# Making the decay tables of a chunked linear attention in place, by VectorE scans

## The chip, the cores and the metric

The kernel runs on one core of a Trainium2 chip. The metric is the device time of one execution in microseconds; the median of several runs is given. All data are float32.

## The reference

Two blocks follow each other. The first is a linear attention with decay (B=4, H=8 heads, S=768, D=64); the second, on the result x of shape (4, 768, 512), adds the real part of a two-dimensional Fourier transform, normalizes the rows and applies an MLP of width 2048. Cut to what matters:

```python
block = 64
rel = pos[:, None] - pos[None, :]
Dmask = np.where(rel >= 0, lam[:, None, None] ** rel[None], 0.0)   # lam: one number a head, 0.97 to 0.99
lam_pow = lam[:, None, None] ** (pos[None, :, None] + 1)
for b in range(nb):                                   # blocks of the sequence
    intra = (qb @ kb.T * Dmask) @ vb
    inter = (qb * lam_pow) @ kv_state
    out[block] = intra + inter
    kv_state = lam ** block * kv_state + (kb * lam ** (block - 1 - pos)).T @ vb
x = out as (B, S, H * D)
u = x + real(fft(fft(x, axis=1), axis=2))
un = (u - mean(u)) / sqrt(var(u) + 1e-6)              # over the 512 columns
result = u + relu(un @ w_ch1) @ w_ch2
```

The result doesn't depend on the block's size. The kernel uses blocks (chunks) of 128, so it needs, for each of the 8 heads h, the powers of lam[h] from 0 to 128.

## The kernel before

**Tables.** Three tables come out of lam. `decay` [128, 8, 128] holds, on partition j, lam[h]^(i-j) for i >= j and 0 else; it multiplies the transposed scores (`sc`, L295), and its last column `kpow` scales k for the state update (`kd`, L269, on GpSimd). `qpow` [128, 4, 128] holds lam[h]^(i+1) for the two heads of a pair, one on partitions 0 to 63 and one on 64 to 127; it multiplies the transposed q (`qs`, L283), and its last column `spow` scales the running state (L310).

They are made in L152 to L188. lam is read into eight partitions (`sq`, L154). VectorE doubles the number of known powers seven times, on eight partitions: a tensor_scalar extends the row `z` by its own length times lam^n (L159), and a tensor_tensor squares lam^n (L161). The row, 127 zeros, then powers 0 to 128, is stored to device memory (`zd`, L165). From there `qpow` is read by two DMAs that repeat a row on 64 partitions (L170), and `shifted` by one whose partitions start one element apart (L182). TensorE multiplies `shifted` by `flip`, the identity with reversed columns (L186), which turns the order of the partitions round, and ScalarE copies the two halves to `decay` (L187).

**Attention, `attn_chunk`.** For each batch, six chunks in order. A chunk loads k, q, v for all heads (L262, two buffers each, so the load of chunk c+2 waits until chunk c has let go of the buffer), transposes k and q on TensorE (L273, L278; copies to `kT`, `qT` by ScalarE, L275, L280), makes scores (L291), masks them (L295), updates the state (L306, L308 to L311), makes the output transposed (L319, L323, copied by L326), turns it back (L330) and copies it to `x` or `xn` (L333, L334). Parts of x are stored to device memory (`xa`, `xb`, L337 to L341), and gathered from there mirrored (L377 to L385, by indirect DMAs of GpSimd) for the fold with which the Fourier transform begins (L366 to L415).

**The rest.** `fft_ln` makes the Fourier transform by matmuls (L439, L452 to L457) and the normalization (L469 to L492). `mlp` runs four of the twelve pairs of row tiles through the two weight matrices (L554, L568), woven with the attention of the later batches; the other eight go through `late` in pairs, with seven products in place of eight (L636, L683).

**Weights.** They are loaded in 32 pieces of 512 KB (`raw`, L228). VectorE and ScalarE unpack each with seven instructions (L233 to L241). `raw` shares its five buffers with the MLP's hidden rows.

**Order.** The loads of k, q, v, `raw` and the tables of the Fourier transform are issued on one queue, SP's; the stores of `xa` and `xb` on ScalarE's. The program is written as generators that yield estimated durations, and `weave` interleaves them in proportion; the first batch's attention is woven with half of the first weight matrix:

```python
run(weave(attn(0), part(w, 0.5 * NW), 0.5 * NW / t_att))
```

Within that, a build-time planner orders each engine's queue, so an instruction need not be issued in its source order; where the order must hold, `keep_in_program_order` says so. [...]

Of the kernel before, what the change touches and what calls it, by code (L numbers as in the profile page):

```python
# [10 lines left out]
F32 = mybir.dt.float32  # L11
# [5 lines left out]
ALU = mybir.AluOpType  # L17
# [59 lines left out]
def kernel(  # L77
# [10 lines left out]
    nc = tc.nc  # L88
    B, H, S, D = q.shape
    DM = H * D  # L90
    DFF = moe_w_ch1.shape[1]
    C = 128
    NC = S // C
    HC = NC // 2
    HP = H // 2
# [10 lines left out]
    HD = [slice(0, 64), slice(64, 128)]  # L106
# [8 lines left out]
    def front_pool(name, bufs):  # L115
        return front_end.enter_context(tc.tile_pool(name=name, bufs=bufs, side="left"))
# [4 lines left out]
    const = front_pool("const", 1)  # L121
# [3 lines left out]
    fp = front_pool("fp", 1)  # L125
# [5 lines left out]
    dram = ctx.enter_context(tc.tile_pool(name="dram", bufs=1, space=bass.MemoryType.DRAM))  # L131
# [7 lines left out]
    def new(pool, shape, tag, **kw):  # L139
        cnt[0] += 1  # L140
        return pool.tile(shape, F32, tag=tag, name=f"{tag}{cnt[0]}", **kw)
# [4 lines left out]
    def psum_m(shape):  # L146
        return new(pm, shape, "pm")
# [1 line left out]

    z = fp.tile([H, 2 * C], F32, tag="fo0", name="z")  # L152
    sq = const.tile([H, 8], F32, name="sq")
    nc.sync.dma_start(sq[:, 0:1], lam.rearrange("(h o) -> h o", o=1))  # L154
    nc.vector.memset(z, 0.0)
    nc.vector.memset(z[:, C - 1:C], 1.0)
    n, b2 = 1, 0
    while n < C:
        nc.vector.tensor_scalar(z[:, C - 1 + n:C - 1 + 2 * n], z[:, C - 1:C - 1 + n],  # L159
                                sq[:, b2:b2 + 1], None, op0=ALU.mult)  # L160
        nc.vector.tensor_tensor(sq[:, b2 + 1:b2 + 2], sq[:, b2:b2 + 1], sq[:, b2:b2 + 1], op=ALU.mult)  # L161
        n, b2 = 2 * n, b2 + 1
    nc.vector.tensor_copy(z[:, 2 * C - 1:2 * C], sq[:, b2:b2 + 1])
    zd = dram.tile([H, 2 * C], F32, name="zd")
    nc.sync.dma_start(zd, z)  # L165
    z0 = zd[0:1, 0:1]

    qpow = const.tile([128, HP, C], F32, name="qpow")
    for hi in range(2):
        nc.sync.dma_start(  # L170
            qpow[HD[hi]],
            bass.AP(z0.tensor, z0.offset + hi * 2 * C + C, [[0, D], [4 * C, HP], [1, C]]))
    spow = qpow[:, :, C - 1:C]

    ident = const.tile([128, 128], F32, name="ident")
    make_identity(nc, ident)


    flip = fp.tile([128, 128], F32, tag="ds", name="flip")
    nc.vector.tensor_copy(flip, ident[:, ::-1])  # L180
    shifted = fp.tile([C, H, C], F32, tag="fe0", name="shifted")
    nc.sync.dma_start(shifted, bass.AP(z0.tensor, z0.offset, [[1, C], [2 * C, H], [1, C]]))  # L182
    decay = const.tile([C, H, C], F32, name="decay")
    for g in range(0, H, 4):
        ps = psum_m([C, 4, C])
        nc.tensor.matmul(ps, lhsT=flip, rhs=shifted[:, g:g + 4, :], start=True, stop=True)  # L186
        nc.scalar.copy(decay[:, g:g + 4, :], ps)  # L187
    kpow = decay[:, :, C - 1:C].broadcast_to([C, H, D])  # L188

    cvt = const.tile([128, 1], F32, name="cvt")  # L190
# [627 lines left out]
```

## Time and profile before

| | us |
|---|---|
| median of 8 runs | 876.17 (873.32 to 881.85) |
| profiled execution | 876.15 |
| its span | 874.4 |
| PE (matmul) busy | 802.0 (92%) |
| DVE busy | 436.1 (50%) |
| ACT busy | 179.1 (20%) |
| POOL busy | 82.5 (9%) |
| mean granted TensorE clock | 0.982 of full speed |

The span runs from the first to the last instruction of the profile; 1.75 us of the execution lie around it. PE is TensorE's matmuls, PEld its weight loads, DVE is VectorE, ACT ScalarE, POOL GpSimd, SP the queue of SyncE. A line such as L295 is a line of the kernel. Where a row of the timeline has a bracket, it gives how long the engine was idle before the instruction, and what ended that. [...]

### The profile page before, as it was taken

How to read it: one execution, taken by the hardware profiler on the slowest of the kernel's cores; microseconds unless marked ns; L12 is line 12 of the kernel's file. 1: busy time of each engine (PE TensorE's matmuls, PEld its weight loads, DVE VectorE, ACT ScalarE, POOL GpSimd, SP SyncE). 2: the span in 40 equal slices, each digit the busy share in tenths (PEclk: the TensorE clock that was granted, in tenths of full speed). 3: DMA queues.
4: the chain of work that ended last, by engine and by line, in shares of the span. 5: the costliest groups of instructions: out<-in, count | busy, mean ns of one | idle time of the engine just before them, and what ended most of it. 6: DMA issues, size and time to landing. Idle time of an engine off the chain costs nothing.

```text
span 874.4 us, 11679 instructions
## 1 busy us (share of the span) xinstructions
PE 802.0 (92%) x4596; PEld 638.7 (73%) x4596; DVE 436.1 (50%) x1022; ACT 179.1 (20%) x419; POOL 82.5 (9%) x107
## 2 busy tenths in 40 slices
PE   4764768789999999999999999999999999999998
PEld 2654657645877567864884888888888888888886
DVE  4776959953652447425597454125611553135411
ACT  3552425520322113211210220012100220012100
POOL 2213211101021202102000000000000000000000
PEclk9996889999999999999999999999999999999999
DMA  8987434811066504642153101110111000110010
GB/s 224 247 217 214 122 121 126 276 51 48 25 128 140 149 25 118 125 97 90 37 138 85 55 1 49 48 49 1 49 37 54 7 1 1 48 49 1 1 37 24
DMA packets 129405, 72.42 MB, mean 83 GB/s; under 512 B 111264, under 2 KB 113832, under 8 KB 129352
## 3 DMA queue, kind: packets, MB, share of 16 engines
q1 hardware_dynamic: 123392, 57.51, 26.0%
q0 software_dynamic: 2496, 7.87, 2.7%
q10 hardware_dynamic: 3464, 6.30, 2.0%
q8 instruction: 36, 0.59, 0.3%
q14 instruction: 17, 0.14, 0.0%
HBM read 50.68 MB, written 20.99 MB: 82 GB/s over the span
## 4 chain that ended last, share of the span: by engine, by line
PE 74%; DVE 9%; DMA 6%; issue 5%; ACT 2%; POOL 1%; ACTq 0%; POOLq 0%; DVEq 0%; SPq 0%
PE p L683 22%; PE p L636 22%; PE pm L554 8%; PE pm L568 8%; PE pa L439 3%; PE pa L323 2%; DMA raw<-in_moe_w_ch_dram 2%; PE pa L291 2%; PE pa L319 1%; DMA xa<-xn 1%; DMA fo<-xa,ix 1%; DMA x<-xb,ix 1%; PE pa L330 1%; DVE sc L295 1%; PE pa L306 1%
## 5 line engine op out<-in xcount | busy, mean ns | idle before, releaser
L554 PE MATMUL pm<-ut,w 128*128 128x256 f32 x512 | 120.9, 384 | 6.1 <-ACT hr L562 6.1
L568 PE MATMUL pm<-w,hr 128*128 128x512 f32 x256 | 114.8, 596 | 0.0
L554 PEld LDWEIGHTS pm<-ut,w 128*128 128x128 f32 x512 | 93.7, 190 | 22.6 <-ACT hr L562 7.6
L636 PE MATMUL p<-ur,w 128*128 128x256 f32 x384 | 93.5, 379 | 0.0
L568 PEld LDWEIGHTS pm<-w,hr 128*128 128x128 f32 x256 | 47.0, 190 | 51.8 <-issue 51.2
L636 PEld LDWEIGHTS p<-ur,w 128*128 128x128 f32 x384 | 73.0, 190 | 10.3 <-issue 0.5
L636 PE MATMUL p<-us,w1s 128*128 128x256 f32 x256 | 65.5, 379 | 0.0
L683 PE MATMUL p<-w,hs 128*128 128x256 f32 x256 | 58.0, 379 | 0.5 <-DVE y L704 0.5
L683 PE MATMUL p<-w2s,hs 128*128 128x256 f32 x256 | 57.9, 379 | 0.0
L683 PE MATMUL p<-w,ha 128*128 128x256 f32 x256 | 57.9, 379 | 0.0
L683 PEld LDWEIGHTS p<-w,hs 128*128 128x128 f32 x256 | 48.5, 190 | 7.5 <-DVE y L704 0.9
L683 PEld LDWEIGHTS p<-w2s,hs 128*128 128x128 f32 x256 | 48.6, 190 | 6.6
L683 PEld LDWEIGHTS p<-w,ha 128*128 128x128 f32 x256 | 48.6, 190 | 6.6
L636 PEld LDWEIGHTS p<-us,w1s 128*128 128x128 f32 x256 | 48.6, 190 | 6.6
L544 POOL DMA_INDIRECT out_dram<-y,ix x12 | 11.8, 984 | 404.6 <-DVE y L709 344.0
L663 ACT COPY ha<-p 128x256 f32<-128x256 f32 x32 | 11.9, 373 | 170.7 <-PE p L636 141.1
L323 PE MATMUL pa<-sc,v 128*64 128x128 f32 x384 | 32.0, 292 | 12.5 <-DVE sc L295 12.5
L291 PE MATMUL pa<-qT,kT 64*128 64x128 f32 x384 | 30.3, 298 | 11.5 <-ACT qT L280 11.5
L291 PEld LDWEIGHTS pa<-qT,kT 64*128 64x128 f32 x384 | 25.3, 198 | 20.6 <-ACT qT L280 17.6
L283 DVE TENSOR_TENSOR qs<-pa,qpow 128x512 f32<-128x512 f32 x20 | 13.8, 689 | 50.1 <-ACT qT L280 50.1
L323 PEld LDWEIGHTS pa<-sc,v 128*64 128x64 f32 x384 | 23.7, 143 | 20.1 <-DVE sc L295 15.8
L295 DVE TENSOR_TENSOR sc<-pa,decay 128x512 f32<-128x512 f32 x48 | 31.1, 681 | 11.7 <-PE pa L291 7.7
(140 smaller groups left out, 1129.6 us busy)
## 6 DMA issues: line engine op xcount, KB each, us to landing
raw<-in_moe_w_ch_dram SPq DMA_DIRECT2D x32, 512.0 KB, 5.1
k<-in_k_dram SPq DMA_DIRECT2D x24, 256.0 KB, 4.4
q<-in_q_dram SPq DMA_DIRECT2D x24, 256.0 KB, 4.3
v<-in_v_dram SPq DMA_DIRECT2D x24, 256.0 KB, 4.0
ud<-x SPq DMA_DIRECT2D x16, 256.0 KB, 2.1
utd<-uq SPq DMA_DIRECT2D x64, 64.0 KB, 2.2
ur<-utd SPq DMA_DIRECT2D x8, 512.0 KB, 5.1
u<-ud SPq DMA_DIRECT2D x16, 256.0 KB, 2.7
```

The source lines that it names most:

```text
L283: nc.vector.tensor_tensor(qs, ptq, qpow, op=ALU.mult)
L291: mm(pss[hi][:, hp, :], lhsT=kT[HD[hi], hp, :], rhs=qT[HD[hi], hp, :], start=True, stop=True)
L295: nc.vector.tensor_tensor(t, pss[hi], decay[:, hi::2, :], op=ALU.mult)
L306: mm(pu[HD[hi], hp, :], lhsT=kd[:, h, :], rhs=vt[:, h, :], start=True, stop=True)
L323: mm(po[HD[hi], hp, :], lhsT=vt[:, 2 * hp + hi, :], rhs=sc[hi][:, hp, :], start=(c == 0 and hp == 0), stop=(hp == HP - 1), skip_group_chec ...
L439: mm = nc.tensor.matmul(ps[0:m, n, :], lhsT=piece(a, i, n), rhs=cs[0:rows, a, i in (2, 3), n, :], start=(a == 0), stop=(a == 1))
L544: nc.gpsimd.indirect_dma_start(out=out.rearrange("b s d -> (b s) d"), out_offset=row_of(2 + HC * (b + 1) + T - HC), in_=y[:, :], in_offset ...
L554: nc.tensor.matmul(ps, lhsT=w1[:, c, 128 * fc:128 * fc + 128], rhs=ut[:, c, :], start=(c == 0), stop=(c == KO - 1))
L568: nc.tensor.matmul(ps, lhsT=hr[fc // 4][:, fc % 4, 128 * i:128 * i + 128], rhs=w2[:, fc, :], start=(fc == 0), stop=(fc == FO - 1))
L636: nc.tensor.matmul(ps, lhsT=s2.A[a][:, kt, 128 * i:128 * i + 128], rhs=U[b][:, kt, :], start=(first and kt == 0), stop=(kt == 1), skip_gro ...
L663: nc.scalar.copy(a11, two(X))
L683: nc.tensor.matmul(ps, lhsT=h[a][:, s, i, :], rhs=s2.B[b][:, i, :], start=(first and i == 0), stop=(i == HF - 1), skip_group_check=True)
```

## The change

The powers are no longer made on eight partitions, stored, read back and turned. lam is read once, with all 128 partitions getting its eight values (`lamb`). A scan of VectorE runs along a row and computes state = (a[i] op0 state) op1 b[i], giving the state at each i. With a = lam repeated, op0 = multiply, op1 = add and b = the identity's row, partition j gets 0 until i = j, then 1, then the powers of lam: that is `decay` of one head, directly where it is used. Eight such scans make the table. `qpow` is made by four scans that start at 1 and only multiply, with `lamq` holding the two heads' lam on the two halves of the partitions. The store `zd`, the three reads from it, `flip`, `shifted`, TensorE's two products and ScalarE's two copies are gone.

```diff
-    z = fp.tile([H, 2 * C], F32, tag="fo0", name="z")
-    sq = const.tile([H, 8], F32, name="sq")
-    nc.sync.dma_start(sq[:, 0:1], lam.rearrange("(h o) -> h o", o=1))
-    nc.vector.memset(z, 0.0)
-    nc.vector.memset(z[:, C - 1:C], 1.0)
-    n, b2 = 1, 0
-    while n < C:
-        nc.vector.tensor_scalar(z[:, C - 1 + n:C - 1 + 2 * n], z[:, C - 1:C - 1 + n],
-                                sq[:, b2:b2 + 1], None, op0=ALU.mult)
-        nc.vector.tensor_tensor(sq[:, b2 + 1:b2 + 2], sq[:, b2:b2 + 1], sq[:, b2:b2 + 1], op=ALU.mult)
-        n, b2 = 2 * n, b2 + 1
-    nc.vector.tensor_copy(z[:, 2 * C - 1:2 * C], sq[:, b2:b2 + 1])
-    zd = dram.tile([H, 2 * C], F32, name="zd")
-    nc.sync.dma_start(zd, z)
-    z0 = zd[0:1, 0:1]
-
-    qpow = const.tile([128, HP, C], F32, name="qpow")
-    for hi in range(2):
-        nc.sync.dma_start(
-            qpow[HD[hi]],
-            bass.AP(z0.tensor, z0.offset + hi * 2 * C + C, [[0, D], [4 * C, HP], [1, C]]))
-    spow = qpow[:, :, C - 1:C]
-
+    lamb = const.tile([128, H], F32, name="lamb")
+    nc.sync.dma_start(lamb, lam.rearrange("(o h) -> o h", o=1).broadcast_to([128, H]))
     ident = const.tile([128, 128], F32, name="ident")
     make_identity(nc, ident)
-    flip = fp.tile([128, 128], F32, tag="ds", name="flip")
-    nc.vector.tensor_copy(flip, ident[:, ::-1])
-    shifted = fp.tile([C, H, C], F32, tag="fe0", name="shifted")
-    nc.sync.dma_start(shifted, bass.AP(z0.tensor, z0.offset, [[1, C], [2 * C, H], [1, C]]))
+    scan = nc.vector.tensor_tensor_scan
+
     decay = const.tile([C, H, C], F32, name="decay")
-    for g in range(0, H, 4):
-        ps = psum_m([C, 4, C])
-        nc.tensor.matmul(ps, lhsT=flip, rhs=shifted[:, g:g + 4, :], start=True, stop=True)
-        nc.scalar.copy(decay[:, g:g + 4, :], ps)
+    for h in range(H):
+        scan(decay[:, h, :], lamb[:, h:h + 1].broadcast_to([C, C]), ident, 0.0, op0=ALU.mult, op1=ALU.add)
+
+    lamq = const.tile([128, HP], F32, name="lamq")
+    for hi in range(2):
+        nc.vector.tensor_copy(lamq[HD[hi]], lamb[HD[hi], hi::2])
+    qpow = const.tile([128, HP, C], F32, name="qpow")
+    for hp in range(HP):
+        scan(qpow[:, hp, :], lamq[:, hp:hp + 1].broadcast_to([128, C]), ident, 1.0, op0=ALU.mult, op1=ALU.bypass)
+    spow = qpow[:, :, C - 1:C]
     kpow = decay[:, :, C - 1:C].broadcast_to([C, H, D])
```

## The prediction

> **What bounds the kernel now.** I read four views, in this order. First the busy times in two long stretches of the span. After the stretch, its length and its end of share, the columns are the busy us (and instructions) of PE, PE's weight loads, DVE, ACT and POOL, then the granted clock, the DMA share and GB/s.
>
> ```profile
> 0.00:180.00 180.00, 120.20 (x1072) 97.12 (x1072) 135.17 (x294) 76.98 (x152) 35.69 (x48) 0.91 0.71 194
> 180.00:874.00 694.00, 681.84 (x3524) 541.62 (x3524) 300.90 (x730) 102.13 (x268) 46.79 (x59) 1.00 0.21 54
> ```
>
> From 180 us on PE is busy 98% of the time: only 12.2 us of idle are left in 694. Before 180 it is idle for 59.8 us. The change sits in the first 20 us, so its worth is the amount by which the steady PE stretch begins earlier: work after it can't be squeezed, but it can be shifted whole.
>
> Second, the timeline of the first 20 us (start, duration, instruction, idle time before it and what ended that).
>
> ```profile
> 0.73 0.41 SPq L154 DMA_DIRECT2D sq<-in_lam_dram  x1
> ...
> 2.16 0.20 DVE L159 TENSOR_SCALAR z<-z,sq 8x1 f32<-8x1 f32 x1 [0.94 <-DMA sq<-in_lam_dram]
> ...
> 5.49 0.30 SPq L165 DMA_DIRECT2D zd<-z  x1
> ...
> 7.47 2.08 PE L291 MATMUL pa<-qT,kT 64*128 64x128 f32 x16 [0.67 <-ACT qT L280]
> 8.22 0.60 SPq L182 DMA_DIRECT2D shifted<-zd  x1
> ...
> 14.25 3.75 PE L186 MATMUL pm<-shifted,flip 128*128 128x512 f32 x4 [4.70 <-DMA shifted<-zd]
> ...
> 18.04 0.59 ACT L187 COPY decay<-pm 128x512 f32<-128x512 f32 x1 [1.12 <-PE pm L186]
> 18.66 1.29 DVE L295 TENSOR_TENSOR sc<-pa,decay 128x512 f32<-128x512 f32 x2 [3.94 <-ACT decay L187]
> 18.71 1.06 POOL L269 TENSOR_TENSOR kd<-k,decay 128x512 f32<-128x512 f32 x1 [15.07 <-ACT decay L187]
> ...
> 19.80 0.38 SPq L262 DMA_DIRECT2D k<-in_k_dram  x1
> ...
> 19.82 0.69 PE L306 MATMUL pa<-v,kd 128*64 128x64 f32 x16 [1.82 <-POOL kd L269]
> ```
>
> The decay table goes lam, DVE steps, store, load, PE, ACT, and is whole at 18.63. The scores of the first chunk left PE at 9.55 (7.47 + 2.08) and lie there until `sc` starts at 18.66. `kd` waits 15.07 us for the same table; since it frees the buffer of k, the third k load leaves SP only at 19.80. So the table, and nothing else, sets when the first chunk ends.
>
> Third, the chain that ended last: it starts at 19.8 and runs chunk after chunk through PE, ACT and DVE with no DMA in it up to 54 us.
>
> ```profile
> 54.35 8.62 DMA xa<-xn
> 63.25 8.54 DMA fo<-xa,ix
> ...
> 164.16 6.04 DMA raw<-in_moe_w_ch_dram
> ```
>
> Here the reader sees where the head start could be lost: transfers in a busy DMA, not PE.
>
> Fourth, the wait list of 60 to 200 us, for the rival below:
>
> ```profile
> PE pa L323 <- DVE sc L295: 10.1, 2, 9.6
> ```
>
> [...] No scan is in this trace. [...]the read of lam, issued at 0.73, lets DVE go at 2.16, so 1.43 us here, and the trace's number is used. [...]PE idles for 9.63 us to 76.30 (clock 0.50 between 72 and 84).
>
> **The change, part by part.** Removed on DVE: two memsets, 14 steps, a copy and `flip`, 0.84 to 5.6. Removed on SP: `zd`, two `qpow`, `shifted`. `zd` had held SP for 2.4 us until the steps were done, so the two `raw` behind it move from 5.83 to about 3.2, and the second chunk's k from 8.87 to about 4.1; 0.78 MB less goes through the DMA (at the 272 GB/s of 14 to 18 us, 2.9 us of traffic). Removed on PE and ACT: 3.75 us of L186 and 2 x 0.59 of L187, both beside idle time, so nothing by themselves.
>
> Added: one DMA of lam to 128 partitions instead of 8, first on SP. It issues in 0.41, as any there; landing I take as 1.6 us (at least the 1.43 of the small one, at most the 3.4 us in which 256 KB of k land, 1.19 to 4.57): 2.35. What is queued behind it on SP, k, q, v, keeps its place.
>
> 12 scans. Neighbouring 128x512 tensor_tensors start 0.60 apart, 128x256 ones 0.33 apart (fold steps at 89.21 and 89.55), so 1.05 ns an element and 0.06 fixed. [...] Bounds: 0.20 at full rate[...]. I take 0.33. The first scan may be slow: two small DVE steps took 1.19 and 1.05 us and ended at 3.65, just as POOL's memsets did (3.64). So the first ends at 3.65, the eighth at 3.65 + 7 x 0.33 = 6.0. Two small copies at 0.2 (as `flip`) and four scans follow: DVE is free at 7.7, and `qpow` (first used by the second chunk) hides behind PE's scores, which end at 9.55. If scans cost 1.1, decay is there at 3.65 + 7.7 = 11.4 and DVE free at 16.2. With 0.20 nothing changes, since q and k are then the late ones.
>
> So decay moves from 18.63 to 6.0, but `sc` can't start before 9.55: of 12.6 us 9.1 can be had. **What is late next** is DVE's own queue: two `raw` pieces land at about 7.5 to 9.5, and unpacking both took from 9.71 to 14.72 in the idle time that goes. If both go ahead of `sc`, from 8.3 on, it starts at 13.3; if none does, at 9.55. That is a gain of 5.4 to 9.1; I take the middle, 7.2. `kd` has its input at 6.0 and costs 1.06 on POOL, free from 3.64: the release of k is then covered.
>
> From there I let the chain shift whole. DMA moved 13.8 MB in the first 60 us (235, 225 and 229 GB/s by 20 us); 7 us earlier and 0.78 MB less is 13.0 in 53 us, 246 GB/s; the trace shows 323 in 8 to 12. The profiled execution took 876.15 us, span 874.4 and 1.75 around it, equal to the median of 876.17. Sum: 876.2 - 7.2 = **869.0 us**.
>
> **The rivals.** *The DMA eats it.* Its share was 0.94, 0.87 and 0.92 in those three stretches, and the store of `xa` took 8.62 us in the queue. If 235 GB/s is what this mix of short packets can do, only the dropped bytes count: 0.78/0.235 = 3.3 us, 872.9. Against it: single stretches at 310 to 330, and no DMA in the chain before 54.
>
> *Slow scans.* At 1.1 us, `sc` starts between 11.4 (before the qpow scans) and 16.2: gain 2.5 to 7.3, middle 4.9, 871.3.
>
> *A new order of queues, slower.* Instructions aren't issued in source order: L186 stands ahead of the first chunk in the source and runs after its L291. With the head changed, the planned order of the front can change too. One place is dear: the next batch's first `sc` stands on DVE behind the fold that waits for a gather, and PE idles 9.6 us (the wait shown). If the second batch gets one more such place, it costs 9.6 and the halved clock after it (here 3.8 us: L323 2.57 for 1.10, L330 1.12 for 0.66, L273 and L278 1.06 for 0.60 each, L291 2.08 for 1.16): 13.4 - 7.2 = 6.2 us slower, 882.4. It decides as soon as more than 7.2 us of new waiting stand in PE's queue before 180.
>
> *It doesn't do what it says*: the table could be early and `sc` still at 18.7 if it waited for `raw`. The trace has its wait end with decay's copy, within 0.03 us, so I give this almost nothing: 876.
>
> **How the numbers follow.** Chances: the shift 0.60; DMA eats it 0.13; slow scans 0.10; new order 0.15; no effect 0.02. A measurement here tells about 0.5% (4.4 us) from no change, so faster means below 871.8. The shift (0.60) and half of the slow scans (0.05) are faster: 0.65. DMA, the other half of the scans and no effect are the same: 0.20. Slower: 0.15. The range: the lower end takes the full 9.1 us, the 2.9 us of dropped traffic where the store of `xa` is in the chain, and something of the old 9.6 us wait: 861. The upper reaches the new order, 883.
>
> **What would show it.** Right: scans of 0.3 to 0.45 us; decay done near 6; `sc` of the first chunk between 9.5 and 13.5; the third k load no later than 12; PE's idle time before its steady stretch down from 59.8 to about 52; that stretch beginning near 173. Wrong: `sc` on time and the steady stretch still near 180 (eaten by DMA: look at the `xa` store), or a new wait of L323 or L319 for DVE of several us before 180 (order).

## The result and the profile after

The changed kernel took 868.88 us (median of 11 runs, 865.0 to 870.4) beside 876.28 for the kernel before: ratio 0.9911, 95% interval 0.9890 to 0.9933. On another chip, beside the last experiments, it gave 870.58 and 0.9936 [0.9914, 0.9959]. So it is faster, by 5.6 to 7.8 us going by the two ratios; 869.0 had been predicted. The profiled execution has a span of 868.2 (874.4 before). Lines of the file are 19 lower than before: L295 is now L276, L291 L272, L306 L287, L323 L304, L330 L311.

The two stretches, with the same columns as before:

```profile
0.00:173.00 173.00, 121.81 (x1069) 99.50 (x1069) 135.97 (x290) 75.54 (x151) 39.66 (x48) 0.92 0.71 197
173.00:868.00 695.00, 683.54 (x3524) 542.43 (x3524) 300.57 (x729) 101.67 (x267) 46.70 (x59) 1.00 0.21 54
```

PE's idle time ahead of the steady stretch went from 59.8 to 51.2 us, and the stretch kept its density (11.5 us idle in 695). PE's busy time, though, is 805.35 us in all where it was 802.04, although 3.75 us of matmuls are gone: up to the first fold it was busy for 41.8 us, where the kernel before took 37.1 without these 3.75. It ran more of its work at half speed, as the durations below show. (Before, at 76.30 us, in a stretch where the granted clock is 0.50 (72 to 84 us), the output product takes 2.57 us; at 27.33 it takes 1.09.)

The timeline of the first 20 us:

```profile
0.73 0.38 SPq L153 DMA_DIRECT2D lamb<-in_lam_dram  x1
...
3.57 1.37 SPq L209 DMA_DIRECT2D raw<-in_moe_w_ch_dram  x2
3.61 0.34 DVE L164 COPY lamq<-lamb 64x4 f32<-64x4 f32 x2 [3.61 <-DMA lamb<-in_lam_dram]
3.99 2.63 DVE L160 TENSOR_TENSOR_SCAN decay<-lamb,ident 128x128 f32<-128x128 f32 x8
...
4.96 1.09 PE L254 MATMUL pa<-ident,k 128*128 128x128 f32 x4 [4.96 <-DMA k<-in_k_dram]
...
6.53 2.16 DVE L167 TENSOR_TENSOR_SCAN qpow<-lamq,ident 128x128 f32<-128x128 f32 x4
6.71 1.08 POOL L250 TENSOR_TENSOR kd<-k,decay 128x512 f32<-128x512 f32 x1 [3.07 <-DVE decay L160]
9.23 0.67 ACT L214 ACTIVATE sg<-raw 128x512 bf16<-128x512 int16 x1 [7.22 <-DMA raw<-in_moe_w_ch_dram]
...
9.80 0.57 ACT L256 COPY kT<-pa 128x512 f32<-128x512 f32 x1
...
10.91 2.08 PE L272 MATMUL pa<-qT,kT 64*128 64x128 f32 x16 [3.70 <-ACT qT L261]
...
12.51 0.38 SPq L243 DMA_DIRECT2D k<-in_k_dram  x1
...
13.68 1.28 DVE L276 TENSOR_TENSOR sc<-pa,decay 128x512 f32<-128x512 f32 x2
```

The table is whole at 6.62 us instead of 18.63. But ACT's `sg`, which waits for `raw` until 9.23, now stands ahead of the copy of kT (which starts at 9.80, though PE was done with its input at 6.05), so the scores start at 10.91 and not at 7.47; and before `sc`, at 13.68, DVE unpacks one piece of `raw` and does three of the five steps of a second. Of 12 us, 5.0 arrived at `sc`.

The chain that ended last now starts with a load of weights, the second, which lands at 10.58; DVE's unpacking and `sc` follow it. Where the chain meets the gather for the first fold it again has two transfers:

```profile
4.51 6.07 DMA raw<-in_moe_w_ch_dram
...
49.49 7.81 DMA k<-in_k_dram
...
57.87 6.33 DMA fo<-xa,ix
```

Before, the gather ran from 63.25 to 71.79. It now ends 7.6 us sooner, more than the 5.0 us that `sc` had gained. In between the lead had been smaller: 4.3 us at the fifth chunk's output (`oT` transposed at 48.37, before at 52.66), and in a second profiled execution only 2.2; at the gather's issue it was 5.4. So the lead is neither made at `sc` alone nor carried on whole. The second weight pass (L549) starts at 175.4, before at 182.1; at the end 6.2 us of span remain.

### The profile page after: what moved, and what is told of

Same layout as the page of the kernel before. It is cut to its first block, busy times and chain, and to the rows that moved or that the text cites. A ratio compares the mean times of both kernels' runs of the same rounds, so it can differ in the third digit from the quotient of the medians.

```text
span 868.2 us, 11653 instructions
## 1 busy us (share of the span) xinstructions
PE 805.3 (93%) x4592; PEld 641.9 (74%) x4592; DVE 436.5 (50%) x1018; ACT 177.2 (20%) x417; POOL 86.4 (10%) x107
## 4 chain that ended last, share of the span: by engine, by line
PE 75%; DVE 11%; DMA 6%; issue 5%; ACT 2%; POOL 1%; SPq 0%; POOLq 0%; DVEq 0%; ACTq 0%
PE p L664 22%; PE p L617 22%; PE pm L535 8%; PE pm L549 8%; PE pa L420 3%; PE pa L304 3%; DMA raw<-in_moe_w_ch_dram 2%; PE pa L272 1%; PE pa L300 1%; PE pa L311 1%; DVE sc L276 1%; DMA x<-xb,ix 1%; DMA fo<-xa,ix 1%; DVE w L221 1%; DMA k<-in_k_dram 1%
## 5 line engine op out<-in xcount | busy, mean ns | idle before, releaser
L535 PE MATMUL pm<-ut,w 128*128 128x256 f32 x512 | 123.2, 390 | 5.0 <-ACT hr L543 5.0
L549 PE MATMUL pm<-w,hr 128*128 128x512 f32 x256 | 116.0, 601 | 0.0
L549 PEld LDWEIGHTS pm<-w,hr 128*128 128x128 f32 x256 | 47.6, 192 | 52.6 <-issue 51.9
L617 PEld LDWEIGHTS p<-ur,w 128*128 128x128 f32 x384 | 73.0, 190 | 10.3 <-issue 0.5
L664 PE MATMUL p<-w,ha 128*128 128x256 f32 x256 | 57.9, 379 | 0.0
L664 PE MATMUL p<-w2s,hs 128*128 128x256 f32 x256 | 57.9, 379 | 0.0
L304 PE MATMUL pa<-sc,v 128*64 128x128 f32 x384 | 33.9, 299 | 10.3 <-DVE sc L276 10.1
L272 PE MATMUL pa<-qT,kT 64*128 64x128 f32 x384 | 29.4, 291 | 11.7 <-ACT qT L261 11.7
L272 PEld LDWEIGHTS pa<-qT,kT 64*128 64x128 f32 x384 | 24.5, 193 | 21.1 <-ACT qT L261 18.1
L304 PEld LDWEIGHTS pa<-sc,v 128*64 128x64 f32 x384 | 25.0, 147 | 18.7 <-DVE sc L276 14.6
L264 DVE TENSOR_TENSOR qs<-pa,qpow 128x512 f32<-128x512 f32 x20 | 13.8, 688 | 46.7 <-ACT qT L261 46.7
L655 DVE TENSOR_TENSOR ha<-p,ha 128x256 f32<-128x256 f32 x32 | 13.6, 424 | 44.2 <-ACT ha L654 44.2
```

Of the source, the lines that this page charges most:

```text
L264: nc.vector.tensor_tensor(qs, ptq, qpow, op=ALU.mult)
L272: mm(pss[hi][:, hp, :], lhsT=kT[HD[hi], hp, :], rhs=qT[HD[hi], hp, :], start=True, stop=True)
L304: mm(po[HD[hi], hp, :], lhsT=vt[:, 2 * hp + hi, :], rhs=sc[hi][:, hp, :], start=(c == 0 and hp == 0), stop=(hp == HP - 1), skip_group_chec ...
L535: nc.tensor.matmul(ps, lhsT=w1[:, c, 128 * fc:128 * fc + 128], rhs=ut[:, c, :], start=(c == 0), stop=(c == KO - 1))
L549: nc.tensor.matmul(ps, lhsT=hr[fc // 4][:, fc % 4, 128 * i:128 * i + 128], rhs=w2[:, fc, :], start=(fc == 0), stop=(fc == FO - 1))
L617: nc.tensor.matmul(ps, lhsT=s2.A[a][:, kt, 128 * i:128 * i + 128], rhs=U[b][:, kt, :], start=(first and kt == 0), stop=(kt == 1), skip_gro ...
```

## The experiments

Theory A was the prediction's own: the end follows the first `sc`. Against it stood the order in which DVE, ACT and SP take their work (apart from the tables' own instructions the two kernels have the same order on PE and POOL, but not on ACT and SP, and least of all on DVE), the traffic that was dropped, and PE's clock. Chunk 1 is the second chunk; its output is the turning back of `oT`. Times of steps below are from one profiled execution each, the ratio from all.

| kernel | first `sc` | chunk 1: k transposes to output | gather issued, fold starts | ratio to before [95%] |
|---|---|---|---|---|
| before | 18.7 | 22.6 to 29.1 | 63.3, 71.8 | 1 |
| after, first / second | 13.7 / 13.9 | 18.6 to 26.4 / 18.8 to 28.1 | 57.9, 64.2 / 58.8, 64.6 | 0.9911 / 0.9936 |
| e1 decay alone | 13.8 | 18.7 to 28.3 | 63.4, 72.5 | 0.9992 [0.9975, 1.0009] |
| e2 qpow alone | 18.1 | 22.1 to 29.2 | 62.9, 67.8 | 1.0020 [1.0004, 1.0036] |
| p1 after, old order | 15.2 | 20.1 to 29.2 | 62.3, 70.3 | 0.9987 [0.9976, 0.9998] |
| p2 before, new order | 18.4 | 24.0 to 33.6 | 66.1, 69.8 | 0.9987 [0.9966, 1.0008] |
| p3 traffic | 14.7 | 18.7 to 28.9 | 63.2, 67.6 | 0.9939 [0.9920, 0.9959] |
| p4 late table | 27.0 | 33.3 to 42.2 | 73.4, 79.5 | 1.0095 [1.0067, 1.0123] |
| e5 ACT pinned | 14.2 | 19.7 to 27.5 | 58.4, 65.2 | 0.9952 [0.9939, 0.9965] |
| e6 `sc` first | 10.4 | 15.3 to 24.5 | 55.9, 63.5 | 0.9944 [0.9923, 0.9966] |
| q1 warm, new order | 14.6 | 19.5 to 27.3 | 58.0, 64.2 | 0.9941 [0.9920, 0.9962] |
| q2 warm, old order | 15.3 | 19.9 to 29.2 | 61.9, 70.3 | 0.9958 [0.9940, 0.9975] |
| q3 warm, `sc` first | 10.3 | 14.2 to 23.7 | 56.8, 64.6 | 0.9939 [0.9924, 0.9954] |

**Half of the change each.** e1 makes `decay` by scans and `qpow` by the steps and device memory; e2 the reverse.

```diff
+    z = fp.tile([H, 2 * C], F32, tag="fo0", name="z")
...
+    nc.sync.dma_start(zd, z)
+    z0 = zd[0:1, 0:1]
+    for hi in range(2):
+        nc.sync.dma_start(
+            qpow[HD[hi]],
+            bass.AP(z0.tensor, z0.offset + hi * 2 * C + C, [[0, D], [4 * C, HP], [1, C]]))
...
-        scan(qpow[:, hp, :], lamq[:, hp:hp + 1].broadcast_to([128, C]), ident, 1.0, op0=ALU.mult, op1=ALU.bypass)
```

That is e1; e2 takes z and zd back likewise, keeps the scans of `qpow`, and has `flip`, `shifted`, L186 and L187 in place of the eight scans.

> decay by scans as in the changed kernel; qpow still made by the seven steps, stored and read back (0.26 MB of the dropped 0.78 MB of DMA traffic stay, and the store still holds SP for some 2.4 us). Theory A, the table's lateness sets the first chunk: the scans run behind the steps, decay is done near 8, sc of the first chunk starts at 13 to 14, the median is 867 to 871, as the changed kernel's 868.9. Theory B, the gain comes from the shorter queue of SP and the dropped traffic: only two thirds of the bytes are gone and SP is still held, so 872 to 875.

> qpow by scans, decay still by steps, device memory, TensorE and ScalarE (0.52 MB of the traffic stay). Theory A: decay is done near 18, sc of the first chunk starts near 18, the median is 875 to 877, as the kernel before. Theory B: a third of the bytes gone, 873.5 to 875.

e1 has its first `sc` at 13.8 us, as the whole change has, and gains nothing that can be told from noise: 875.05 us. So an early `sc` isn't enough, and A as it stood falls. The order of e1 is neither kernel's: SP's queue is the old one, ACT's all but an instruction, DVE's lies between the two. e2, whose table is late, is at 876.18.

**The order alone and the table alone.** p1 is the changed kernel with the order of DVE, ACT and SP of the kernel before, p2 the kernel before with the changed kernel's order.

```diff
+    by = {i.name: i for i in nc.cur_bb.bb.instructions}
+    for chain in order.values():
+        names = ["I-" + n for n in chain.split()]
+        for a, b in zip(names, names[1:]):
+            tc.add_manual_dep(by[b], a, mybir.DependencyInfo(
+                mybir.DependencyClass.NoSync, mybir.DependencyReason.DATA), reason="order")
```

`order` holds, for each of the three engines, the names of its first instructions (175, 110 and 62) in the other kernel's order.

> The changed kernel with its queues of DVE, ACT and SP bound, over the stretch in which they differ, to the order of the kernel before (apart from the table's own instructions). Theory A, the table's lateness: 868 to 870. Theory O, the gain is the new order that the planner chose, and the early table is lost later: 874 to 877. Theory T, the dropped traffic and SP not held by the store: 868 to 870.

> The mirror: the kernel before, its tables made by steps, memory, TensorE and ScalarE, with the queues of DVE, ACT and SP bound to the order of the changed kernel. Theory A: 875 to 878, perhaps more, since kT then waits for raw. Theory O: 868 to 871. Theory T: 875 to 877.

The early table alone (p1) and the new order alone (p2) each measure 0.13%, p1 just clear of none and p2 not; together they are worth 0.64 to 0.89%, more than the sum. Where p1 loses its 3.5 us at `sc` is seen in the timeline of its PE, from the first chunk's output to the second's:

```profile
15.96 2.57 PE L304 MATMUL pa<-sc,v 128*64 128x128 f32 x16 [5.00 <-DVE sc L276]
...
22.70 2.08 PE L272 MATMUL pa<-qT,kT 64*128 64x128 f32 x16 [0.67 <-ACT qT L261]
24.71 1.12 PE L287 MATMUL pa<-v,kd 128*64 128x64 f32 x16
25.76 1.76 PE L300 MATMUL pa<-qs,st 64*64 64x128 f32 x16
27.46 1.09 PE L304 MATMUL pa<-sc,v 128*64 128x128 f32 x16
29.24 0.66 PE L311 MATMUL pa<-ident,oT 128*128 128x128 f32 x4 [0.69 <-ACT oT L307]
```

The kernel before did the same work in these stretches at full speed:

```profile
20.34 1.05 PE L323 MATMUL pa<-sc,v 128*64 128x128 f32 x16
...
24.61 1.16 PE L291 MATMUL pa<-qT,kT 64*128 64x128 f32 x16 [1.01 <-ACT qT L280]
25.70 0.69 PE L306 MATMUL pa<-v,kd 128*64 128x64 f32 x16
26.31 1.09 PE L319 MATMUL pa<-qs,st 64*64 64x128 f32 x16
...
29.11 0.66 PE L330 MATMUL pa<-ident,oT 128*128 128x128 f32 x4 [0.69 <-ACT oT L326]
```

In chunk 1 no wait is longer in p1; the instructions are (2.08 for 1.16, 1.12 for 0.69, 1.76 for 1.09). From k's transposes to the output chunk 1 takes 9.1 us instead of 6.5, from `sc` to those transposes 4.9 instead of 3.9, and both kernels transpose chunk 1's output at 29.1 to 29.2. p2 runs chunk 1 at half speed too (2.08 us for the scores, 1.12 for the state products), in 9.6 us, and is 4.5 us behind the kernel before at its end; it gets that back at the first step of the fold, where its gather takes 3.73 us from issue to use, not 8.56.

What goes with a fast gather shows in the two queues. Before (SP's loads, then POOL's gather):

```profile
61.32 0.37 SPq L262 DMA_DIRECT2D v<-in_v_dram  x1
61.80 2.40 SPq L228 DMA_DIRECT2D raw<-in_moe_w_ch_dram  x2
```

```profile
63.25 1.27 POOL L377 DMA_INDIRECT fo<-xa,ix  x1 [9.59 <-DMA xa<-xn]
```

After:

```profile
50.60 4.43 SPq L209 DMA_DIRECT2D raw<-in_moe_w_ch_dram  x1
57.56 0.37 SPq L243 DMA_DIRECT2D v<-in_v_dram  x1
58.03 0.52 SPq L209 DMA_DIRECT2D raw<-in_moe_w_ch_dram  x1
```

```profile
57.87 1.17 POOL L358 DMA_INDIRECT fo<-xa,ix  x1 [8.47 <-DMA k<-in_k_dram]
```

In the old order v and two loads of weights (256 KB and twice 512) are issued about when the gather comes, in the new one v and one load, beside the rest of a load issued by 55.03. The packets in the traces say how far the gather stands behind them: between its issue and its own first packet 248 of the weights' 4 KB packets move before and 142 after (a load has 128), which puts the first packet 5.5 and 3.2 us after the issue. The fourteen profiles agree: the gather's first part takes 8.0 to 9.1 us with v and two loads ahead of or just beside it (before, e1, p1, q2), 5.9 to 7.8 where the first load of weights is issued 0.1 to 1.1 us after it (the changed kernel twice, e5, e6, q1, q3, p4), 3.7 to 4.9 where that comes 1.3 us or more after it (e2, p2, p3). No run moved these loads alone, so this is a relation across kernels and not an isolated test.

Nor is a sooner fold yet a sooner end. e2's and p2's first fold step comes 4.0 and 2.0 us ahead of the kernel before, and neither is faster by its median. Their chains that ended last go through the gather's second part (64.80 to 71.99, and 67.61 to 74.22) and not through its first. Also, e2's profiled execution was 2.6 us faster than its median and p2's 2.9 us slower, so these rows are not the usual execution. What of the new order's worth lies in the gather stays open.

**How much `sc` and the traffic matter in the new order.** Both kernels keep the changed kernel's order, bound as above. p4 passes lam through five small copies in device memory before `lamb` is read; p3 adds three loads with the shapes of `qpow` and `shifted` (0.77 MB), read from q and used by nobody, ahead of the second chunk's k.

```diff
-    nc.sync.dma_start(lamb, lam.rearrange("(o h) -> o h", o=1).broadcast_to([128, H]))
+    hop = lam.rearrange("(o h) -> o h", o=1)
+    for i in range(5):
+        nxt = dram.tile([1, H], F32, name=f"hop{i}")
+        nc.gpsimd.dma_start(nxt, hop)
+        hop = nxt[0:1, :]
+    nc.gpsimd.dma_start(lamb, hop.broadcast_to([128, H]))
```

```diff
+        if b == 0 and c == 1:
...
+            for hi in range(2):
+                nc.sync.dma_start(junk2[HD[hi]], bass.AP(qf.tensor, qf.offset + hi * 2 * C + C, [[0, D], [4 * C, HP], [1, C]]))
+            nc.sync.dma_start(junk, bass.AP(qf.tensor, qf.offset, [[1, C], [2 * C, H], [1, C]]))
```

> The changed kernel in its own order, with lam reaching the scans late: it is copied five times through device memory on GpSimd's queue before it is read with 128 partitions, so that decay is done near 18 as before, without the old traffic, TensorE or ScalarE work; the scans stand behind the first unpacking on DVE. Theory A: 875 to 878. Theory O: 868 to 871. Theory T: 868 to 871.

> The changed kernel in its own order, with three loads added on SP between the second weight piece and the second chunk's k, in number, shape and bytes those of the dropped qpow and shifted (0.77 MB), from q, used by nothing. Theory A: 868 to 870. Theory O: 868 to 870. Theory T: 872 to 876.

p4's table, meant to be there near 18, was whole only at 26.8. Its `sc` comes 13.3 us later than in the changed kernel and the end 14 to 16 us later (1.0095 less 0.9936 or 0.9911, of 876). With p2 (4.7 us later, 4.5 to 6.7 lost) that is about one for one: in this order lateness at `sc` does reach the end, as A said. p3 stands 0 to 2.5 us above the changed kernel's two measurements: by the medians the dropped bytes were worth at most 2.5 us.

**Still earlier.** e5 pins the first `sg` behind the copies of kT and qT on ACT; e6 also runs the first chunk alone up to `sc` and pins the first unpacking on DVE behind it.

```diff
+        first = nc.scalar.activation(sg, top.bitcast(I16), AF.Sign)
+        if not pinned:
+            pinned.append(tc.keep_in_program_order(first))
```

```diff
+        first = nc.vector.tensor_scalar(pw, top, 0x7FF0, None, op0=ALU.bitwise_and)
+        if len(pinned) == 1:
+            pinned.append(tc.keep_in_program_order(first))
...
+    a0 = attn(0)
+    run(part(a0, 2.7))
```

> The changed kernel with one more order: on ScalarE the sign of the first weight piece (which waits for raw until 9.2) stands behind the copies kT and qT of the first chunk, not in front of them. Theory A, the wait that took the place of the old one is ScalarE's: the scores L272 start near 7.5 in place of 10.9, sc near 12 in place of 13.7, and the end follows: 866 to 867.5. Rival C, what is late next is DVE's unpacking or the DMA queue: the scores are early, sc is not, or the second chunk isn't, and the median stays within 1 us of 868.9.

> As e5_act_pin, and the first weight piece comes after the first chunk's sc in the source, so that sc stands on DVE before most of the unpacking; the second piece is loaded after the second chunk's k, q, v. Theory A: sc of the first chunk near 10, second chunk's transposes near 14.5 in place of 18.6, 864 to 866.5. Rival C: the weights are later by about 2 us and the DMA eats the rest: 868 to 871.

In e5 the scores start at 7.8 instead of 10.9, but `sc` only at 14.2: DVE's unpacking alone holds it. The time, 871.13, is no better than the changed kernel's, and outside what C had given (within 1 us of 868.9). In e6 `sc` starts at 10.4, 3.3 us ahead of the changed kernel, and the end doesn't move (870.35). Its chunk 1 takes 9.2 us; what lead is left at the fifth output (46.89 against 48.37 and 50.47) goes in part in the gather, 7.62 us where the changed kernel's took 6.36 and 5.85, and the 0.7 to 1.1 us that are left at the fold don't reach the end.

**PE's clock.** If half speed in chunk 1 is what eats the lead, unread matmuls in PE's idle time might bring the clock up sooner. That is an estimate of mine, from the kernel before, where chunk 0's state products, behind the 3.75 us of L186, take 0.69 us, and from p1, which has no L186, where they take 1.12. c_after is the changed kernel again; q1 is it with two of them before the first scores, q2 is p1 with two after the state products, where L186 used to be, and q3 is e6 with one.

```diff
+        if b == 0 and c == 0:
+            warm = pm.tile([C, DM], F32, tag="pm", name="warm")
+            for _ in range(2):
+                tc.keep_in_program_order(mm(warm, lhsT=ident, rhs=kt.rearrange("p h d -> p (h d)"), start=True, stop=True))
```

> The changed kernel, unaltered, on the chip of the next three, as their yardstick. Both theories: ratio to the kernel before 0.989 to 0.995, about 869 us, scores scaled (sc) of the first chunk at 13.7 us, second chunk's k transposes at 18.6 us, steady stretch (second weight pass) from 175.4 us.

> The changed kernel with its own order of work bound, and two matmuls 128x512 more, whose product nobody reads, on PE between the transposes of q and the first scores, where PE is idle from 7.2 to 10.9 us. Clock theory (the step matmuls that the change removed had also brought PE to its full clock for chunk 1): full clock by about 14.5 us instead of 21, the chunk output of chunk 0 and the transposes of chunk 1 at half their durations, second chunk's transposes at 17 us or sooner, end 2 to 3 us sooner: about 866 us, ratio 0.988. Rival (chunk 1 waits for its raw decays and loads, not for PE): no change, 869 us, ratio 0.991 to 0.993. If the end does not follow a chunk 1 that is sooner, the lead is given back in the fold stretch: also 869.

> The scans in the old order of DVE, ACT and SP (as in p1_after_old_order, 874.0 us), and two unread matmuls 128x512 more on PE after the state products of chunk 0, where PE is idle from 10.9 to 15.9 us: about the place and the length of the step matmuls that were removed. Clock theory: full clock by about 18 us instead of 27, chunk 1 takes 6.5 us from its k transposes to its output as in the kernel before, and not 9.1; the 3.5 us lead of the first sc is kept to the end: 871 to 872 us, ratio 0.995 to 0.996. Rival (the old order alone loses the lead): 874 us, ratio 0.998 to 1.

> The kernel with the first attention run alone up to sc (as in e6_sc_first, 870.4 us; sc at 10.4 us), and one unread matmul 128x512 more on PE before the first scores. Clock theory: scores some 1.2 us later, sc at about 11.5, full clock by 16 to 18 us instead of 22.7, chunk 1 not slower than chunk 2, end at 866 to 867 us, ratio 0.988 to 0.989. Rival (raw decays of chunk 1 come too late whatever PE does, or the lead is lost in the fold stretch): 870 us or more, ratio 0.993 and up.

q1's PE:

```profile
6.93 2.62 PE L272 MATMUL warm<-k,ident 128*128 128x512 f32 x4
11.13 1.16 PE L276 MATMUL pa<-qT,kT 64*128 64x128 f32 x16 [1.59 <-ACT qT L261]
12.22 0.69 PE L291 MATMUL pa<-v,kd 128*64 128x64 f32 x16
15.37 2.57 PE L308 MATMUL pa<-sc,v 128*64 128x128 f32 x16 [2.46 <-DVE sc L280]
```

The clock came up, as the scores' 1.16 us shows, and was down again after the wait for `sc`; the output product ran cold (2.57 us), chunk 1 was no sooner, and the time is the changed kernel's (0.9941 beside 0.9936). q2 fared alike: the start of its output product ran fast (two matmuls in 0.43 us), most of the rest slowly (fourteen in 1.63 us; 1.09 in q3), and chunk 1 takes 9.3 us, as in p1 (9.1). Its ratio, 0.9958, lies where the clock theory had put it, but its profile doesn't show the mechanism, and the same kernel differed by 0.0025 between two measurements here; I don't count it. Only q3 kept PE at full speed from 10.2 us on through chunk 1's output product (0.69 us for the state products, 0.60 for k's transposes, 1.16 for the scores); it had chunk 1's transposes at 14.2 and its fifth output at 47.16, and still ended with the others (870.58), its gather having taken 7.79 us. At full speed chunk 1 took 9.5 us, since its `sc` stood on DVE behind the unpacking:

```profile
16.23 1.16 PE L282 MATMUL pa<-qT,kT 64*128 64x128 f32 x16 [1.00 <-ACT qT L267]
...
19.14 1.55 DVE L227 SCALAR_TENSOR_TENSOR w<-raw,w 128x512 f32<-128x512 uint32 x1
...
20.61 1.28 DVE L286 TENSOR_TENSOR sc<-pa,decay 128x512 f32<-128x512 f32 x2
21.35 0.43 PE L314 MATMUL pa<-sc,v 128*64 128x128 f32 x2 [1.98 <-DVE sc L286]
```

The scores are there at 17.4 and `sc` comes 3.2 us later.

So half speed explains where p1's lead goes, but its being gone earlier (q3) isn't worth anything once `sc` is at 10: there DVE is what chunk 1 waits for. That L186 had kept PE warm is not shown: of the three kernels that have it, two run the products after it at full speed (the kernel before and e2, 0.69 us for the state products) and p2 at half (1.12), and q2's stand-in warmed PE for a few matmuls only. Why one execution has the full clock in chunk 1 and another not stays open.

## Why the prediction was right, and where it wasn't

The time was right. Its steps were not all.

- **Scans**: 0.33 us each predicted; 2.63 us for eight, 0.33 from start to start. Right, though 0.33 was my estimate, without a scan to go by, and the 1.1 of the slow rival no more than an assumption. Measured, one scan of 128 elements takes 0.40 us; in the kernel before a 128x255 tensor_tensor takes 0.41 and the next starts 0.34 after it (89.21, 89.55). `decay` was whole at 6.62, not 6.0, since lam landed at 3.61 (2.35 predicted) and DVE put the two `lamq` copies first, so that the first scan began at 3.99, when it should have ended by 3.65.
- **Order on SP**: `raw` at 3.57 (3.2 predicted), second k at 4.99 (4.1): 0.4 and 0.9 late, since v and the two pieces of `raw` took longer to issue (1.27 and 1.37 us, before 0.93 and 0.82). Third k load at 12.51; "no later than 12" was missed.
- **`sc`**: 9.55 to 13.3 predicted, 13.68 measured, so 5.0 us of gain and not the middle, 7.2. The mis-sized term is the unpacking ahead of it: eight of the ten steps of the two pieces and not half of them, begun at 9.23 and not at 8.3. I also held the scores' end at 9.55 although ACT's queue, too, had `raw` work that could step ahead of kT; they ended at 12.99. DVE's queue as "what is late next" was right: e5 freed ACT and gained nothing.
- **"From there I let the chain shift whole"**: this step failed. The lead of 5.0 shrank to 4.3 (2.2 in the second execution) by the fifth output and was 7.6 (7.2) after the gather. p1 shows that in the old order hardly any of it (0.13%) would have arrived.
- **L186 and L187 "nothing by themselves"**: their going could not be shown to cost anything (above). PE's busy time rose all the same.
- **The rivals**: the new order of queues was real, and it decided the result. I had given it one mechanism and one sign, a second wait like that for the fold, slower by 6.2; the new one has fewer weights ahead of the gather instead, which goes with a faster gather but isn't shown to be all that it does. DMA eating the lead was wrong for this change and right for the next step: e6 and q3 lose theirs partly in that gather. Slow scans and no effect are out.

So that 869.0 fits is luck. It came from two errors that cancelled: 2.2 us too much at `sc` and a lead taken as constant, against 3.3 us up to the fold that I hadn't seen (4.3 to 7.6; in the second execution 5.0). Of these, 1.1 come before the gather's issue and 2.2 in the gather; 1.4 are lost again by the end of the span. From the store of `xa`, where I said to look, to the gather's issue it took 8.1 us (8.9 before); what ended that wait was by the profile the store before, and the load of k after.

## What to carry to other kernels

When a head of a kernel is made shorter, compare the order of every queue before and after as well: here the early table and the new order measured 0.13% each, and only both together 0.6 to 0.9%. A lead is to be followed from stage to stage (first `sc`, each chunk, the gather, the steady stretch), not taken over whole. Where the main engine waits for a gather, look at which bulk loads on the other queues are issued ahead of it; moving them alone is the run that is missing here.

## What the runs showed of the hardware

The work ahead of PE's turn to full speed was of very different length. In q1 PE worked from 4.92 to 9.55 and did the scores at 11.13 in 1.16 us; after the wait of 2.46 us for `sc` it was at half speed again (2.57 us for the output product). In the second execution of the changed kernel PE worked from 11.18 on with waits of at most 0.68 us and turned fast only near 26:

```profile
11.18 2.08 PE L272 MATMUL pa<-qT,kT 64*128 64x128 f32 x16 [4.04 <-ACT qT L261]
...
14.66 2.57 PE L304 MATMUL pa<-sc,v 128*64 128x128 f32 x16 [0.35 <-DVE sc L276]
...
24.46 1.97 PE L300 MATMUL pa<-qs,st 64*64 64x128 f32 x16
26.36 1.10 PE L304 MATMUL pa<-sc,v 128*64 128x128 f32 x16
```

The granted clock in the view of stretches reads 1.00 from 0 to 29 us of this execution, so half speed had to be read from the durations here. In q1 the view reads 0.50 from 18 to 21 us, where k's transposes take 1.06 us as well. A read of eight numbers into 128 partitions took 2.9 us from issue to landing (0.73 to 3.61), the same into eight partitions 1.43 (0.73 to 2.16, in the kernel before).
